# Where VectorE's transposes of K put odd and even keys in a grouped-query attention kernel

## The chip, the cores and the metric

The kernel runs on one core of a Trainium2 chip. The metric is device time in microseconds of one execution, the median of the runs shown. The engines are named as in the profile: PE is TensorE (PEld its weight loads), DVE is VectorE, ACT is ScalarE, POOL is GpSimd, and SP issues DMAs.

## The reference

Attention with 32 query heads and 8 key/value heads, batch 16, 16 query rows, 2048 keys and a head dimension of 128, all in bf16. Four query heads share one key/value head, so one key/value head serves 4 x 16 = 64 query rows.

```python
B, Hq, Hkv, Sq, Sk, D = 16, 32, 8, 16, 2048, 128
k = jnp.repeat(k, rep, axis=1)
v = jnp.repeat(v, rep, axis=1)
scores = jnp.einsum("bhqd,bhkd->bhqk", q, k) * D ** -0.5
p = softmax(scores, axis=-1)
out = jnp.einsum("bhqk,bhkd->bhqd", p, v)
```

## The kernel before

The 16 x 8 = 128 key/value heads are taken in 64 pairs (`NP`), and everything loops over the pairs. The two heads of a pair have 128 query rows together, one per partition.

**Loads.** SP issues everything in one order (line 176 K, line 184 V, line 196 Q, line 204 stores): for each pair 1 MB of K into one of six buffers `Kn`, 1 MB of V into one of eight buffers `Vb`, five pairs behind K, and the store of a finished pair twelve pairs behind. A K load waits until VectorE has transposed what the buffer held; a V load waits until TensorE has used it. In `Kn` each partition `a` holds 32 successive keys, 32 x 128 bf16, seen as 64 f32 words per key (a word is two neighbouring bf16). The key within the partition is split as (x, t, e): x is the half, t one of eight blocks, e even or odd.

**Transposes of K.** VectorE's function `kt` (line 317) transposes 32x32 blocks of these f32 words from `Kn` into `KT`, two instructions per pair of heads, one for each x, so that the head dimension comes to stand on the partitions. For each of 8 t and 2 b (which half of the head dimension) the block of 128 words in `KT` before the change is ordered (e, a, x): all even keys, then all odd keys, and within each the 32 partitions a with x alternating. One instruction writes one x, so its 32 results of a block go to every second word.

**Scores.** TensorE (line 268, and line 224 for matmuls on weights that are already loaded) multiplies Q by `KT` into `S_ps`, 2048 columns in four banks, in the column order in which `KT` has the keys. `S_ps` exists once, so the scores of the next pair wait until VectorE has emptied it. VectorE (line 333) multiplies by the negative scale, writes `Sneg` in SBUF (f32) and takes the row minimum into `nbias`.

**Exponential.** ScalarE (line 368) computes P = exp(nbias - Sneg) in bf16 with the row sum. P must have the even and the odd key of one place next to each other, because two bf16 are then taken as one f32 word and transposed together by TensorE (line 280) and copied out by ScalarE (line 378) as `PT`. Since `Sneg` has them 64 columns apart, the exponential's input is read with a step: for each of 16 blocks `n` and 64 places `y`, first e = 0, then e = 1, while the output is written in order.

**Output.** TensorE multiplies `PT` by V into `O_ps` (line 298, line 304 for the last twelve pairs), three pairs behind; ScalarE divides by the row sum (lines 391 and 395; VectorE at line 348 for the last pair), from the reciprocal that VectorE takes at line 324. Q is spread by GpSimd (line 165), transposed by TensorE (line 246) and copied by ScalarE (line 358), once in eight pairs, in four parts.

The order of the work is written out by hand in `pe_prog` and `act_prog`: scores of pair p + 1, exponential of p, output of p - 3, transposes of P of p. On VectorE the order of a pair is the evacuation of p, the reciprocal of p - 1, and the two transposes of K of p + 2; there are two buffers each of `KT`, `Sneg` and `P`. The engines wait for each other on semaphores that count: `sem_kt` the transposes of K, `sem_s` the scores, `sem_max` the evacuations, `sem_exp` the exponentials.

## Time and profile before

| | |
|---|---|
| median of 3 runs | 344.95 us (344.94 to 345.17) |
| profiled execution | 344.92 us, its span 343.1 us |
| PE busy | 312.1 us, 91% of the span |
| DVE busy | 297.6 us, 87% |
| ACT busy | 291.8 us, 85% |
| POOL busy | 30.3 us, 9% |
| DMA | 138.94 MB, mean 405 GB/s |
| HBM | 136.31 MB read, 2.10 MB written |
| granted TensorE clock | 1.00 |

The span runs from the first to the last instruction of the profiled execution; the time also holds what lies around it. A row of the page's groups names the line, the engine and the operation, what it writes and reads with the shapes, and how often; then its busy time in us and the mean ns of one; then the idle time of its engine just before such instructions and what ended most of it. In a timeline a row begins with the start and the duration in us; "x2" are two instructions shown as one row, and what stands in brackets is the idle time before it and its releaser.

### The profile page before, as it was taken

The page shows a single profiled execution, that of the slowest core. Times are in us where ns is not written, and L with a number is a line of the kernel's source. Part 1 is how long each engine was busy: PE and PEld are TensorE (multiplying, and loading weights), DVE is VectorE, ACT ScalarE, POOL GpSimd, SP SyncE. Part 2 cuts the span into 40 slices and gives each one's busy share as a digit, 9 for nine tenths or more (in the row PEclk, how much of TensorE's full clock was granted, in tenths as well). Part 3 has the DMA queues.
Part 4 walks back from the last instruction along what each step waited for, and adds up shares of the span by engine and source line. Part 5 has one row for each costly group of instructions (what it writes and reads, how often), then busy time and mean ns, then how long its engine had stood idle before and what let it go on. Part 6 is the DMA issues. An engine that isn't in the chain of part 4 may idle for free.

```text
span 343.1 us, 8217 instructions
## 1 busy us (share of the span) xinstructions
PE 312.1 (91%) x3904; PEld 189.2 (55%) x2880; DVE 297.6 (87%) x321; ACT 291.8 (85%) x404; POOL 30.3 (9%) x15
## 2 busy tenths in 40 slices
PE   0757999999999999999999999999999999887784
PEld 0413656655665575557555755665565575454354
DVE  2289989999999999999899989998999898989840
ACT  1258899999999999999999999999988899877864
POOL 4500012000400004000300004000040000000000
PEclk9999999999999999999999999999999999999999
DMA  7999999999999999999999999999999999999993
GB/s 294 429 414 415 415 411 413 414 416 417 412 418 419 413 415 417 412 420 415 412 421 414 414 416 416 415 418 417 415 412 419 419 412 420 417 413 418 410 393 126
DMA packets 37300, 138.94 MB, mean 405 GB/s; under 512 B 11408, under 2 KB 11664, under 8 KB 29072
## 3 DMA queue, kind: packets, MB, share of 16 engines
q1 hardware_dynamic: 37264, 138.42, 99.6%
q8 instruction: 27, 0.44, 0.5%
q14 instruction: 9, 0.07, 0.1%
HBM read 136.31 MB, written 2.10 MB: 403 GB/s over the span
## 4 chain that ended last, share of the span: by engine, by line
PE 83%; DMA 5%; issue 4%; DVE 3%; ACT 1%; SPq 1%; POOL 1%; DVEq 0%; ACTq 0%
PE O_ps L298 28%; PE S_ps L268 18%; PE S_ps L224 15%; PE ST_ps L280 15%; PE ST_ps L246 5%; DMA Vb<-in_v_dram 4%; DVE KT L317 2%; PE O_ps L304 2%; DMA Qn<-in_q_dram 1%; DVE Sneg L333 1%; POOL Q L165 1%; SPq L204 1%; ACT P L368 1%; SPq L184 0%; PE S_ps L304 0%
## 5 line engine op out<-in xcount | busy, mean ns | idle before, releaser
L333 DVE TENSOR_SCALAR_CACHE_REDUCE Sneg<-S_ps 128x2048 f32<-128x2048 f32 x64 | 146.2, 2285 | 25.2 <-PE S_ps L224 24.0
L368 ACT ACTIVATE P<-Sneg,nbias 128x2048 bf16<-128x2048 f32 x64 | 158.8, 2481 | 7.7 <-DVE Sneg L333 6.1
L317 DVE STREAM_TRANSPOSE KT<-Kn 128x1024 f32<-128x1024 f32 x128 | 150.9, 1218 | 10.9 <-DMA Kn<-in_k_dram 10.9
L268 PE MATMUL S_ps<-KT,QT 32*64 32x512 bf16 x1024 | 103.4, 391 | 5.5 <-DVE Sneg L333 4.7
L224 PE MATMUL S_ps<-KT,QT 32*64 32x512 bf16 x1024 | 102.0, 385 | 0.0
L298 PEld LDWEIGHTS O_ps<-Vb,PT 128*128 128x128 bf16 x832 | 77.3, 98 | 44.0 <-issue 35.7
L298 PE MATMUL O_ps<-Vb,PT 128*128 128x256 bf16 x832 | 99.9, 273 | 1.5 <-issue 1.5
L378 ACT ACTIVATE PT<-ST_ps 128x512 f32<-128x512 f32 x128 | 69.5, 595 | 6.0 <-PE ST_ps L280 4.8
L280 PE MATMUL ST_ps<-ident,P 128*128 128x128 f32 x512 | 69.0, 278 | 2.8 <-ACT P L368 2.8
L268 PEld LDWEIGHTS S_ps<-KT,QT 32*64 32x64 bf16 x1024 | 30.0, 104 | 70.4 <-issue 61.6
L280 PEld LDWEIGHTS ST_ps<-ident,P 128*128 128x128 f32 x512 | 55.1, 141 | 12.1 <-ACT P L368 9.6
L391 ACT ACTIVATE O<-O_ps,rrec 64x128 bf16<-64x128 f32 x104 | 37.7, 363 | 15.8 <-PE O_ps L298 14.7
L165 POOL COPY Q<-Qn 128x4096 bf16<-128x4096 bf16 x8 | 28.8, 3602 | 224.2 <-PE ST_ps L246 143.9
L246 PE MATMUL ST_ps<-ident,Q 128*128 128x128 f32 x128 | 20.4, 291 | 10.1 <-POOL Q L165 10.1
L358 ACT ACTIVATE QT<-ST_ps 128x512 f32<-128x512 f32 x32 | 19.3, 603 | 10.0 <-PE ST_ps L246 10.0
L246 PEld LDWEIGHTS ST_ps<-ident,Q 128*128 128x128 f32 x128 | 16.4, 150 | 10.1 <-issue 10.1
L304 PE MATMUL O_ps<-Vb,PT 128*64 128x128 bf16 x288 | 9.8, 220 | 7.2 <-issue 7.2
L304 PEld LDWEIGHTS O_ps<-Vb,PT 128*64 128x64 bf16 x288 | 8.5, 110 | 12.9 <-issue 12.9
L324 DVE RECIPROCAL rrec<-rowsum 128x1 f32<-128x1 f32 x64 | 10.1, 158 | 3.1 <-ACT P L368 3.1
L368 ACT ACTIVATION_READ_ACCUMULATOR P<-Sneg,nbias 128x1 f32 x64 | 12.2, 190 | 0.0
L395 ACT ACTIVATE O<-O_ps,rrec 128x128 bf16<-128x128 f32 x9 | 3.3, 365 | 6.6 <-PE O_ps L304 6.6
L333 DVE DVE_READ_ACCUMULATOR Sneg<-S_ps 128x1 f32 x64 | 5.3, 83 | 0.0
(12 smaller groups left out, 10.2 us busy)
## 6 DMA issues: line engine op xcount, KB each, us to landing
Kn<-in_k_dram SPq DMA_DIRECT2D x64, 1024.0 KB, 15.9
Vb<-in_v_dram SPq DMA_DIRECT2D x63, 1024.0 KB, 17.7
Qn<-in_q_dram SPq DMA_DIRECT2D x8, 256.0 KB, 15.6
out_dram<-O SPq DMA_DIRECT2D x64, 32.0 KB, 15.9
Vb<-in_v_dram SPq DMA_DIRECT2D x1, 768.0 KB, 13.0
Vb<-in_v_dram SPq DMA_DIRECT2D x1, 256.0 KB, 12.5
```

The lines of the kernel that those rows point to most:

```text
L165: gp.tensor_copy(Q4[:, :, :, :, :].rearrange("p j b r x -> p (j b) r x"), src.unsqueeze(2).to_broadcast([128, 16, 4, 64]),).then_inc(sem_q ...
L224: return pe.add_instruction(mybir.InstMatmult(name=nc.get_next_instruction_name(), engine=mybir.EngineType.PE, ins=[pe.lower_ap(rhs), pe.l ...
L246: ins = pe.transpose(dst[:, 128 * j:128 * (j + 1)], src[:, 4 * x + j, b, :], ident4[:, :])
L268: ins = pe.matmul(s_ap, w, x, start=(acc == 0), stop=(acc == 3))
L280: ins = pe.transpose(dst[:, 128 * t:128 * (t + 1)], P[p % 2][:, 128 * x:128 * (x + 1)], ident4[:, :])
L298: ins = pe.matmul(O_ps[:, 0:256], pt[:, j // 2, j % 2, :], Vb[p % NV][:, :, j, :], start=(j == 0), stop=(j == J - 1),)
L304: ins = pe.matmul(o_ap(p)[64 * g:64 * (g + 1), :], pt[:, j // 2, j % 2, 64 * g:64 * (g + 1)], Vb[p % NV][:, g, j, :], start=(j == 0), stop ...
L317: dve.transpose(KT[p % NKT][:, :].rearrange("p (t b e a x) -> p x e t b a", t=J // 2, b=2, e=2, x=2)[:, x, :, :, :, :], Kn[p % NK][:, :].b ...
L333: dve.tensor_scalar(Sneg[p % 2][:, :].rearrange("p (t h x) -> p h t x", t=8, h=2), S_ps[:, :].rearrange("p (h t x) -> p h t x", t=8, h=2), ...
L368: act.activation(P[p % 2][:, :].bitcast(BF16).rearrange("p (n y e) -> p n y e", n=16, e=2), Sneg[p % 2][:, :].rearrange("p (n e y) -> p n ...
L378: act.activation(PT[p % NPT][:, 4 * h:4 * (h + 1), :].rearrange("p t q -> p (t q)"), stage_ap(u), ACT.Copy,).then_inc(sem_ev, 1)
L391: ins = act.activation(Osb[p % NO][rows, :], O_ps[rows, 128 * g:128 * (g + 1)], ACT.Copy, scale=rrec[rows, p:p + 1])
```

## The change

The words of a block in `KT` change their order from (e, a, x) to (a, x, e): the even and the odd key of one place are now neighbours. One transpose, which has one x, thus writes the 32 results of a block to every fourth word instead of every second, and goes through its region once for e = 0 and once for e = 1; the compiled instruction writes 2 x 512 elements instead of 2 x 16 x 32. Scores and `Sneg` take the order from `KT`, so the exponential reads `Sneg` and writes `P` straight through, 2048 elements. The number and the order of the instructions on every engine, the waits and the DMAs stay as they are. TensorE's access pattern on `KT` stays too.

```diff
             def kt(p, x):
                 dve.wait_ge(sem_k[p % NK], 16 * (p // NK + 1))
                 dve.transpose(
-                    KT[p % NKT][:, :].rearrange("p (t b e a x) -> p x e t b a", t=J // 2, b=2, e=2, x=2)[:, x, :, :, :, :],
+                    KT[p % NKT][:, :].rearrange("p (t b a x e) -> p x e t b a", t=J // 2, b=2, e=2, x=2)[:, x, :, :, :, :],
                     Kn[p % NK][:, :].bitcast(F32).rearrange("p (x t e b c) -> p x e t b c", x=2, e=2, b=2, c=32)[:, x, :, :, :, :],
                 ).then_inc(sem_kt, 1)
...
                     act.activation(
-                        P[p % 2][:, :].bitcast(BF16).rearrange("p (n y e) -> p n y e", n=16, e=2),
-                        Sneg[p % 2][:, :].rearrange("p (n e y) -> p n y e", n=16, e=2), ACT.Exp,
+                        P[p % 2][:, :].bitcast(BF16), Sneg[p % 2][:, :], ACT.Exp,
                         bias=nbias[:, p:p + 1], scale=-1.0, accum_out=rowsum[:, p:p + 1],
                     ).then_inc(sem_exp, 1)
```

## The prediction

> **What bounds the kernel now.** I read the page's groups of instructions first, to see what the two edited lines cost.

> ```profile
> L333 DVE TENSOR_SCALAR_CACHE_REDUCE Sneg<-S_ps 128x2048 f32<-128x2048 f32 x64 | 146.2, 2285 | 25.2 <-PE S_ps L224 24.0
> L368 ACT ACTIVATE P<-Sneg,nbias 128x2048 bf16<-128x2048 f32 x64 | 158.8, 2481 | 7.7 <-DVE Sneg L333 6.1
> L317 DVE STREAM_TRANSPOSE KT<-Kn 128x1024 f32<-128x1024 f32 x128 | 150.9, 1218 | 10.9 <-DMA Kn<-in_k_dram 10.9
> L378 ACT ACTIVATE PT<-ST_ps 128x512 f32<-128x512 f32 x128 | 69.5, 595 | 6.0 <-PE ST_ps L280 4.8
> L391 ACT ACTIVATE O<-O_ps,rrec 64x128 bf16<-64x128 f32 x104 | 37.7, 363 | 15.8 <-PE O_ps L298 14.7
> ```

> The two VectorE rows lie on one straight line: (2285 - 1218) / 1024 = 1.042 ns an element and a fixed 151 ns. So the transposes, which now write with a step of two f32 (8 bytes), pay nothing for it that the unstepped evacuation does not pay. ScalarE's exponential is the opposite: 2481 ns for 2048 elements, while its rows for 512 and 128 elements give (595 - 363) / 384 = 0.604 ns an element.

> Next the DMA: the page's share of the queue, and the stretches by engine, whose columns are the busy time of PE, PEld, DVE, ACT and POOL, the granted clock, the DMA share and GB/s.

> ```profile
> q1 hardware_dynamic: 37264, 138.42, 99.6%
> 40.00:80.00 40.00, 40.00 (x480) 24.23 (x344) 37.72 (x41) 37.51 (x54) 3.60 (x1) 1.00 1.03 415
> 240.00:280.00 40.00, 38.49 (x457) 23.32 (x327) 36.27 (x41) 36.04 (x53) 3.60 (x1) 1.00 1.02 415
> 320.00:330.00 10.00, 7.22 (x132) 4.51 (x108) 7.31 (x9) 6.50 (x11) 0.00 (x0) 1.00 1.03 409
> ```

> The DMA engines are busy throughout at a flat 415 GB/s, and 138.42 MB at that rate take 333.5 us. TensorE has no idle time in the middle, because it starts late: its first scores come at 14.5 us. From 240 us it has idle time again, and in 320:330 it is busy for 7.22 of 10 us. It has caught up with the loads and waits for them. The timeline of the tail says the same:

> ```profile
> 326.19 1.66 SPq L189 DMA_DIRECT2D Vb<-in_v_dram  x2
> ...
> 339.30 1.09 PE L304 MATMUL S_ps<-Vb,PT 128*64 128x128 bf16 x32 [0.73 <-DMA Vb<-in_v_dram]
> 340.53 0.35 DVE L348 TENSOR_SCALAR O<-S_ps,rrec 128x128 bf16<-128x128 f32 x1 [3.92 <-PE S_ps L304]
> ```

> The last V was issued at 326.19 us and landed 13 us later, behind about 5 MB of other transfers; its matmuls waited for it, and after them come only one evacuation and one store. Today's floor is the loads. Compute lies close under it, and the third view shows how close for VectorE: the start, where it is the bound by itself.

> ```profile
> 24.87 0.16 DVE L324 RECIPROCAL rrec<-rowsum 128x1 f32<-128x1 f32 x1
> 24.94 2.35 DVE L317 STREAM_TRANSPOSE KT<-Kn 128x1024 f32<-128x1024 f32 x2
> 27.22 2.25 DVE L333 TENSOR_SCALAR_CACHE_REDUCE Sneg<-S_ps 128x2048 f32<-128x2048 f32 x1
> 29.40 0.08 DVE L333 DVE_READ_ACCUMULATOR Sneg<-S_ps 128x1 f32 x1
> 29.40 0.16 DVE L324 RECIPROCAL rrec<-rowsum 128x1 f32<-128x1 f32 x1
> ```

> From 24.87 to 29.40 VectorE never idles: one pair of KV heads costs it 4.53 us (two transposes, one evacuation, one reciprocal). In the middle TensorE sets the pace: in the chain of waits the output matmuls of successive pairs start at 140.00, 144.76, 149.41, 154.60 and 159.75 us, so 4.65 to 4.76 us a pair, or 5.15 to 5.19 us in the four of eight pairs that also transpose Q. The loads allow one pair in 333.5 / 64 = 5.21 us. VectorE therefore has 0.68 us a pair of room against the loads.

> **The change, part by part.** It adds and removes no instruction, wait or DMA, and the order on every engine stays. TensorE's reads of KT have the same addresses and the same step as before; only which key stands in which column differs. So the line-268 matmuls, the evacuation and the 32-bit transposes of P cost what they cost. Two access patterns differ.

> *The exponential* (64 times). It read two elements 64 f32 apart, then went back; now it walks straight through. Its new time is bounded by the ScalarE rows: from above by four evacuations of 512, 4 x 595 = 2380 ns, from below by 363 + 1920 x 0.604 = 1523 ns. I take the middle, 1950 ns: 0.5 us off each, 34 us of ScalarE's 292 us in all. On the path this is worth nothing: ScalarE is busy 37.5 of 40 us in the middle stage, and what it would release earlier is TensorE, which itself runs ahead of the loads from 240 us on. In the tail the last exponential ends at 336.31 us and its transposes follow, but the last matmuls stand until 339.30 us for V. Gain at the end: 0.

> *The transposes of K* (128 times). Within one instruction the 32 results of a block went to every second f32; now they go to every fourth, and the instruction passes over the whole region twice, once for even and once for odd keys. Compared by address: the 1024 results were spread over 8 KB in one pass; now there are two passes of 8 KB each, 512 results each, one per 16 bytes. No row of the trace shows a VectorE write with a 16-byte step, so this is the unknown cost, bounded from both sides. Below: 1218 ns. It can't be less, since the number of elements is the same and both VectorE rows already lie on the same 1.042 ns an element. Above: two passes at the price of the present one, 2 x 1218 = 2436 ns. The exponential is the nearest row of a stream with far-apart neighbours in SBUF: against its bounds above it pays (2481 - 2380) / 2048 = 0.05 to (2481 - 1523) / 2048 = 0.47 ns an element, in the middle 0.26. On a transpose that would be +0.05 to +0.48 us, in the middle +0.27. But that row reads, and its two interleaved streams each return to neighbouring words, four to 16 bytes; the new write never returns to a neighbour within a pass. I therefore take the upper end without the fixed part, which one instruction pays once: 151 + 2 x 1067 = 2285 ns, +1.067 us on each.

> [...]

> The cover goes quickly. With d more per transpose a pair costs VectorE 4.53 + 2d. Waiting behind a transpose are, on VectorE, the next pair's evacuation, and behind that TensorE's next scores, which wait for S_ps to be emptied, and ScalarE's exponential. The first evacuation begins at 18.17 us (the four transposes before it have 5.66 to 18.17 us, and even four of 2.285 us fit). Then 62 cycles with transposes follow. After the start of evacuation 62: that evacuation 2.25, scores of pair 63 2.2, its evacuation 2.3, exponential with its accumulator 2.2, transposes and their evacuation 1.9, matmuls 1.2, norm 0.7, store 2.2: 15 us. So the span is the larger of the loads' 343.1 us and

> 18.2 + 62 x (4.53 + 2d) + 15.

> It passes 343.1 at d = 0.23 us, a transpose of 1.45 us. For d = 1.067: 18.2 + 62 x 6.66 + 15 = 446.1 us. TensorE needs at most 5.19 us of each 6.66, and the loads 5.21, so neither is late; K loads would then wait for VectorE to free their buffers. The profiled execution took 344.92 us for a span of 343.1, so 1.8 us lie around it (the median of the runs is 344.95, the same): 447.9 us, **forecast 448 us**. The upper end of 2436 ns (d = 1.22) gives 467 us; with a tail and cycle a little shorter than mine, 445. That is this case's own range.

> **Rivals.**
> 1. *The step costs VectorE only what the exponential pays now.* d = 0.27: 18.2 + 62 x 5.07 + 15 = 347.5, 349 us; at d = 0.48, 375 us. For it: the exponential's row, the only one in the trace. Against it: that is a read that comes back to its neighbours. A transpose between 1.45 and 1.8 us would show it.
> 2. *The step costs VectorE nothing.* d = 0: the sum gives 314 us, far under the loads; time stays at 344.9 us, since the exponential's 34 us lie behind the loads. For it: the present 8-byte step is free.
> 3. *Faster: the loads flow better.* SP's queue holds its loads behind stores that wait for ScalarE: 19.2 us at the norms of line 391. With the exponential 0.5 us shorter the norms come earlier. If the DMA rate rose from 415 to the best of the middle slices, 421 GB/s, 320 us x 6 / 421 = 4.6 us would go: 340 us. It decides only while a transpose stays under 1.45 us. Against it: the queue is busy 99.6% already and 5 MB wait at the end, so earlier issue shortens no transfer.

> **How the numbers follow.** Transposes at about double, 448 us: 0.54. Rival 1, 345 to 382 us: 0.20, of which 0.02 stays within the bound for no change. Rival 2, 344.9 us: 0.18. Rival 3, 340 us: 0.08. About 0.2%, 0.7 us, is what a measurement of this kernel can tell from no change. So slower 0.54 + 0.18 = 0.72, same 0.18 + 0.02 = 0.20, faster 0.08. To hold 8 in 10 the range must reach from the unchanged case to the doubled one: 344.5 to 456 us leaves out rival 3 and the top of the doubled case, some 0.05.

> **What would show it.** The mean of the line-317 row decides: near 2285 ns for the forecast, with VectorE near 100% busy from 20 us on, pairs every 6.7 us, the DMA share falling to about 333 / 446 = 75%, and waits of SP at line 176 for the transposes. The exponential's row should be 1.5 to 2.4 us in every case; if it stays at 2481, the change does not do what it says for ScalarE. A transpose of 1218 ns with a changed time would refute the account of the loads; a slow transpose with an unchanged time would refute the VectorE sum.

## The result and the profile after

The changed kernel takes 406.94 us (median of 6 runs, 405.05 to 407.17) against 345.06 us in the same comparison: ratio 1.178, 95% interval 1.175 to 1.180, so 62 us slower. Its profiled execution took 407.02 us, with a span of 405.2 us; again 1.8 us lie around the span.

The page's group rows after the change, with the DMA queue's row ahead of them:

```profile
q1 hardware_dynamic: 37264, 138.42, 90.2%
...
DVE 71%; issue 21%; PE 5%; DMA 1%; POOL 1%; ACT 0%; SPq 0%; DVEq 0%; ACTq 0%
...
L317 DVE STREAM_TRANSPOSE KT<-Kn 128x1024 f32<-128x1024 f32 x128 | 247.1, 2003 | 5.6 <-DMA Kn<-in_k_dram 5.6
...
L333 DVE TENSOR_SCALAR_CACHE_REDUCE Sneg<-S_ps 128x2048 f32<-128x2048 f32 x64 | 145.0, 2266 | 7.2 <-PE S_ps L224 7.1
L368 ACT ACTIVATE P<-Sneg,nbias 128x2048 bf16<-128x2048 f32 x64 | 128.1, 2002 | 19.3 <-DVE Sneg L333 17.4
```

The transposes went from 1218 to 2003 ns and the exponential from 2481 to 2002 ns; the evacuation stayed. The chain that ended last, which ran through TensorE for 83% of the span before, now lies 71% in VectorE. The stretches by engine (columns PE, PEld, DVE, ACT, POOL, granted clock, DMA share, GB/s) show one engine without a gap and the loads slowed:

```profile
120.00:160.00 40.00, 32.84 (x390) 21.17 (x283) 40.00 (x35) 28.61 (x45) 3.60 (x1) 1.00 1.00 360
360.00:380.00 20.00, 14.38 (x256) 8.97 (x208) 20.00 (x17) 11.99 (x18) 0.00 (x0) 0.99 0.80 299
```

Why the loads are slow is in SP's own waits: its K loads wait for a buffer that VectorE has not yet transposed.

```profile
SPq L176 <- DVE KT L317: 260.7, 58, 10.3
```

It was 53.4 us in 24 waits before. A K load takes 5.3 us from issue to landing (median), where it took 15.9; that fits fewer transfers ahead of it in the queue.

```profile
Kn<-in_k_dram SPq DMA_DIRECT2D x64, 1024.0 KB, 5.3
```

The DMA share did not fall with the rate: it is 1.00 from 120 to 160 us at 360 GB/s, and was 1.03 before at 415. The share alone thus does not show that the loads are at their limit. VectorE's timeline gives the new cycle, from evacuation to evacuation:

```profile
30.25 2.28 DVE L333 TENSOR_SCALAR_CACHE_REDUCE Sneg<-S_ps 128x2048 f32<-128x2048 f32 x1
...
32.53 3.85 DVE L317 STREAM_TRANSPOSE KT<-Kn 128x1024 f32<-128x1024 f32 x2
36.26 2.29 DVE L333 TENSOR_SCALAR_CACHE_REDUCE Sneg<-S_ps 128x2048 f32<-128x2048 f32 x1
...
38.55 3.87 DVE L317 STREAM_TRANSPOSE KT<-Kn 128x1024 f32<-128x1024 f32 x2
42.27 2.27 DVE L333 TENSOR_SCALAR_CACHE_REDUCE Sneg<-S_ps 128x2048 f32<-128x2048 f32 x1
```

A pair takes 42.27 - 36.26 = 6.01 us, against 4.53 before. The first evacuation starts at 18.15 us and evacuation 62 at 390.31 us, so the mean of all 62 cycles is 6.00 us, and 14.9 us follow: 18.15 + 62 x 6.00 + 14.9 = 405.2 us, the whole span.

### The profile page after: what moved, and what is told of

Its sections match the earlier page's. It is cut to its first block, busy times and chain, and to the rows that moved or that the text cites. A ratio compares the mean times of both kernels' runs of the same rounds, so it can differ in the third digit from the quotient of the medians.

```text
span 405.2 us, 8217 instructions
## 1 busy us (share of the span) xinstructions
PE 318.5 (79%) x3904; PEld 199.4 (49%) x2880; DVE 384.9 (95%) x321; ACT 262.2 (65%) x404; POOL 30.3 (7%) x15
## 3 DMA queue, kind: packets, MB, share of 16 engines
q1 hardware_dynamic: 37264, 138.42, 90.2%
## 4 chain that ended last, share of the span: by engine, by line
DVE 71%; issue 21%; PE 5%; DMA 1%; POOL 1%; ACT 0%; SPq 0%; DVEq 0%; ACTq 0%
DVE KT L317 36%; DVE Sneg L333 34%; DMA Qn<-in_q_dram 1%; PE S_ps L268 1%; DVE rrec L324 1%; PE S_ps L224 1%; PE ST_ps L246 1%; POOL Q L165 1%; PE S_ps L304 1%; PE ST_ps L280 1%; PE O_ps L304 1%; ACT QT L358 0%; SPq L176 0%; DVE O L348 0%; ACT P L368 0%
## 5 line engine op out<-in xcount | busy, mean ns | idle before, releaser
L317 DVE STREAM_TRANSPOSE KT<-Kn 128x1024 f32<-128x1024 f32 x128 | 247.1, 2003 | 5.6 <-DMA Kn<-in_k_dram 5.6
L268 PE MATMUL S_ps<-KT,QT 32*64 32x512 bf16 x1024 | 111.6, 403 | 73.1 <-DVE Sneg L333 63.4
L333 DVE TENSOR_SCALAR_CACHE_REDUCE Sneg<-S_ps 128x2048 f32<-128x2048 f32 x64 | 145.0, 2266 | 7.2 <-PE S_ps L224 7.1
L368 ACT ACTIVATE P<-Sneg,nbias 128x2048 bf16<-128x2048 f32 x64 | 128.1, 2002 | 19.3 <-DVE Sneg L333 17.4
L224 PE MATMUL S_ps<-KT,QT 32*64 32x512 bf16 x1024 | 112.1, 399 | 0.0
L268 PEld LDWEIGHTS S_ps<-KT,QT 32*64 32x64 bf16 x1024 | 37.1, 106 | 138.3 <-issue 131.3
L298 PE MATMUL O_ps<-Vb,PT 128*128 128x256 bf16 x832 | 99.9, 273 | 0.0
L298 PEld LDWEIGHTS O_ps<-Vb,PT 128*128 128x128 bf16 x832 | 77.2, 98 | 42.3 <-issue 34.0
L390 ACT ACTIVATE O<-O_ps,rrec 64x128 bf16<-64x128 f32 x104 | 37.7, 363 | 89.3 <-PE O_ps L298 88.7
L280 PE MATMUL ST_ps<-ident,P 128*128 128x128 f32 x512 | 67.9, 276 | 0.9 <-ACT P L368 0.8
L280 PEld LDWEIGHTS ST_ps<-ident,P 128*128 128x128 f32 x512 | 58.1, 142 | 5.6 <-issue 2.5
L304 PEld LDWEIGHTS O_ps<-Vb,PT 128*64 128x64 bf16 x288 | 8.8, 114 | 6.6 <-issue 6.6
L368 ACT ACTIVATION_READ_ACCUMULATOR P<-Sneg,nbias 128x1 f32 x64 | 12.0, 187 | 0.0
L324 DVE RECIPROCAL rrec<-rowsum 128x1 f32<-128x1 f32 x64 | 9.5, 148 | 2.3 <-ACT P L368 2.3
L304 PE MATMUL O_ps<-Vb,PT 128*64 128x128 bf16 x288 | 10.2, 226 | 0.0
L333 DVE DVE_READ_ACCUMULATOR Sneg<-S_ps 128x1 f32 x64 | 4.7, 73 | 0.0
```

The costliest lines, as they stand in the source:

```text
L224: return pe.add_instruction(mybir.InstMatmult(name=nc.get_next_instruction_name(), engine=mybir.EngineType.PE, ins=[pe.lower_ap(rhs), pe.l ...
L268: ins = pe.matmul(s_ap, w, x, start=(acc == 0), stop=(acc == 3))
L280: ins = pe.transpose(dst[:, 128 * t:128 * (t + 1)], P[p % 2][:, 128 * x:128 * (x + 1)], ident4[:, :])
L298: ins = pe.matmul(O_ps[:, 0:256], pt[:, j // 2, j % 2, :], Vb[p % NV][:, :, j, :], start=(j == 0), stop=(j == J - 1),)
L304: ins = pe.matmul(o_ap(p)[64 * g:64 * (g + 1), :], pt[:, j // 2, j % 2, 64 * g:64 * (g + 1)], Vb[p % NV][:, g, j, :], start=(j == 0), stop ...
L317: dve.transpose(KT[p % NKT][:, :].rearrange("p (t b a x e) -> p x e t b a", t=J // 2, b=2, e=2, x=2)[:, x, :, :, :, :], Kn[p % NK][:, :].b ...
```

## The experiments

**Each half alone.** The transposes alone in the new layout:

```diff
-  KT[...].rearrange("p (t b e a x) -> p x e t b a", ...)
+  KT[...].rearrange("p (t b a x e) -> p x e t b a", ...)
   (exponential as before)
```

> Only the transposes' new layout; the exponential keeps its old pattern, so the keys it puts together are not those that V expects. Theory (VectorE sets the pace, ScalarE's gain is off the path): transposes near 2003 ns, exponential near 2481 ns, a pair every 6.0 us, time 407 us as with the whole change. Rival (the shorter exponential gave time back in the changed kernel): up to 62 x 0.48 = 30 us more, 437 us.

Measured: 406.88 us (median), ratio 1.179 (1.177 to 1.181). VectorE's timeline in the profiled run:

```profile
30.93 3.85 DVE L317 STREAM_TRANSPOSE KT<-Kn 128x1024 f32<-128x1024 f32 x2
...
36.90 3.86 DVE L317 STREAM_TRANSPOSE KT<-Kn 128x1024 f32<-128x1024 f32 x2
...
42.89 3.88 DVE L317 STREAM_TRANSPOSE KT<-Kn 128x1024 f32<-128x1024 f32 x2
```

The pairs are 5.97 and 5.99 us apart, and the exponential takes 2502 ns. The mean of the transposes is 2194 ns here, not the 2003 expected: in this profile all VectorE records lengthen in the course of the run, the accumulator reads as well (269 ns in the mean, 83 before the change), while the starts keep their distance, 5.99 us in the mean of all 62 cycles. Why the records lengthen is open; the distance is what is used here. The whole loss comes from the transposes, and the 0.48 us that each exponential saves gives nothing back: 406.88 with the slow one, 406.94 with the fast one.

The exponential alone read straight through:

```diff
   (transposes as before)
-  P[...].bitcast(BF16).rearrange("p (n y e) -> p n y e", n=16, e=2),
-  Sneg[...].rearrange("p (n e y) -> p n y e", n=16, e=2), ACT.Exp,
+  P[...].bitcast(BF16), Sneg[...], ACT.Exp,
```

> Only the exponential reads straight through; the transposes stay, so even and odd keys are not brought together as V expects. Theory (the loads are the floor): exponential 2002 ns, transposes 1218 ns, time 345 us within 0.7. Rival 3 of the prediction (the loads flow better when the stores wait less): 340 us.

Measured: 344.99 us, ratio 0.9994 (0.9985 to 1.0003). The group rows:

```profile
L317 DVE STREAM_TRANSPOSE KT<-Kn 128x1024 f32<-128x1024 f32 x128 | 151.2, 1220 | 16.6 <-DMA Kn<-in_k_dram 16.0
L333 DVE TENSOR_SCALAR_CACHE_REDUCE Sneg<-S_ps 128x2048 f32<-128x2048 f32 x64 | 145.9, 2280 | 20.3 <-PE S_ps L224 20.2
L368 ACT ACTIVATE P<-Sneg,nbias 128x2048 bf16<-128x2048 f32 x64 | 128.2, 2003 | 7.1 <-DVE Sneg L333 5.7
L390 ACT ACTIVATE O<-O_ps,rrec 64x128 bf16<-64x128 f32 x104 | 37.7, 362 | 42.4 <-PE O_ps L298 41.8
```

ScalarE works 31 us less and the time does not move. ScalarE's idle time in front of the norms (the division by the row sum), where it waits for TensorE's output matmuls, grows from 15.8 to 42.4 us; VectorE's wait for K loads in front of the transposes grows from 10.9 to 16.0 us. Is TensorE the floor, then, rather than the loads? Before, it was busy without a gap from 180 to 240 us. Here it is not (columns as above):

```profile
180.00:240.00 60.00, 56.53 (x670) 35.66 (x483) 54.02 (x57) 47.73 (x74) 3.60 (x1) 1.00 1.03 416
```

TensorE catches up with the loads sooner and has 3.5 us of idle time in this stretch, the DMA rate is the 416 GB/s of before, and the end stays where it was: the loads are the floor. SP's waits for the norms of `O_ps` fell from 19.2 to 14.8 us, as rival 3 had it, but the rate did not rise and the time did not fall. Rival 3 is refuted.

**How much slower transposing the loads would hide.** Every second or every fourth pair in the changed form, the others as before (the change in words):

```diff
+  KT in "(t b a x e)" order and the exponential straight if p % K4 == 0, else as before   # K4 = 4, 2
```

> Every fourth pair in the changed form (transposes and exponential), the others as before. Theory (larger of the loads' floor and 18.2 + 62 c + 15, c = mean VectorE cycle = 4.53 + 0.25 x 1.47 = 4.90 us): the sum gives 337 us, under the loads' 343.1, so the slow transposes are hidden and the time stays at 345 us. Rival (each slow transpose costs its length at the end): a quarter of the loss, 345 + 62 / 4 = 360 us.

> Every second pair in the changed form. Theory: c = 4.53 + 0.5 x 1.47 = 5.27 us, 18.2 + 62 x 5.27 + 15 + 1.8 = 361 us. Rival (each slow transpose costs its length): half the loss, 376 us.

Measured: 347.90 us with every fourth pair (ratio 1.0064, 1.0040 to 1.0089), 364.25 us with every second (1.0551, 1.0527 to 1.0576). Both lie far from the rival's 360 and 376 us, but somewhat above the theory: the first 2.9 us above the expected 345, the second 2.5 us above its sum, 18.2 + 62 x 5.27 + 15 + 1.8 = 361.7 us. Of the ten runs of the first, four took 345.53 to 345.85 us, as expected, and six 347.81 to 348.68 us. What parts them is open. The profile is of one of the six, 348.54 us; VectorE's timeline in it:

```profile
201.10 2.25 DVE L335 TENSOR_SCALAR_CACHE_REDUCE Sneg<-S_ps 128x2048 f32<-128x2048 f32 x1
...
206.10 2.29 DVE L335 TENSOR_SCALAR_CACHE_REDUCE Sneg<-S_ps 128x2048 f32<-128x2048 f32 x1 [0.39 <-PE S_ps L225]
...
211.19 2.29 DVE L335 TENSOR_SCALAR_CACHE_REDUCE Sneg<-S_ps 128x2048 f32<-128x2048 f32 x1 [0.44 <-PE S_ps L225]
213.48 3.94 DVE L318 STREAM_TRANSPOSE KT<-Kn 128x1024 f32<-128x1024 f32 x2
217.24 2.30 DVE L335 TENSOR_SCALAR_CACHE_REDUCE Sneg<-S_ps 128x2048 f32<-128x2048 f32 x1
```

Before 206.10 and 211.19 VectorE waits for TensorE's scores; the pair with the slow transposes, 211.19 to 217.24, then costs 6.05 us, which VectorE sets. So VectorE sets some pairs here and TensorE others. Eight pairs, 190.52 to 231.00 us, take 40.48 us, 5.06 a pair where the mean of VectorE's own cycles is 4.90; 18.2 + 62 x 5.06 + 15 = 346.9 us, beside the measured span of 346.8. The threshold that the prediction set at a cycle of 5.00 us thus holds in this profile for the cycle that results, not for the mean of VectorE's work. With every second pair the profile has 5.31 us in the mean of 62 cycles, where the sum had 5.27, and 15.4 us after them.

**What in the write is slow.** A stretch is here four f32 words side by side, 16 bytes. The step of the write varied from pair to pair (the change in words); the sixth form keeps 4 words but writes the even and the odd half of each block in turn, not in two passes over the region.

```diff
-  KT as "(t b e a x)"
+  KT as "(t b e x a)", "(t b e a x)", "(t b a x e)", "(t a b x e)", "(u a v b x e)" for p % 6 = 0 to 4
+  KT as "(t b a x e)", iterated t e b a instead of e t b a, for p % 6 = 5
```

> The transposes of K write with steps of 1, 2, 4, 8 and 16 words by turns of the pair, and every sixth pair with 4 words but the even and odd halves of each block written one after the other instead of in two passes over the whole region; the keys come out in other columns, so only durations count. Theory A (a result pays when it does not share its 16-byte stretch with its neighbour): 1218, 1218, 2003, 2003, 2003 ns, and 2003 for the sixth. Theory B (the address walked is paid, as the prediction's doubling supposed): 2003 at step 4, and more at each doubling, 3.5 us at 8. Theory C (the second pass over words already half written is what costs): the sixth form, which comes back after 64 results, differs from 2003.

Measured: 380.29 us in one run. The transposes of pairs 0 to 5 in VectorE's timeline, two to a row, with steps of 1, 2, 4, 8, 16 and the sixth form:

```profile
5.65 2.37 DVE L327 STREAM_TRANSPOSE KT<-Kn 128x1024 f32<-128x1024 f32 x2 [5.65 <-DMA Kn<-in_k_dram]
9.36 2.37 DVE L327 STREAM_TRANSPOSE KT<-Kn 128x1024 f32<-128x1024 f32 x2 [1.33 <-DMA Kn<-in_k_dram]
...
20.39 3.85 DVE L327 STREAM_TRANSPOSE KT<-Kn 128x1024 f32<-128x1024 f32 x2
...
26.58 3.93 DVE L327 STREAM_TRANSPOSE KT<-Kn 128x1024 f32<-128x1024 f32 x2
...
32.63 3.65 DVE L327 STREAM_TRANSPOSE KT<-Kn 128x1024 f32<-128x1024 f32 x2
...
38.67 3.85 DVE L327 STREAM_TRANSPOSE KT<-Kn 128x1024 f32<-128x1024 f32 x2
```

The later turns of the six forms repeat these rows within 0.1 us. Theory A holds. Steps of 1 and 2 words are alike, from 4 words on the price is there and does not grow, and the order of the two halves changes nothing. The address walk, with which the prediction reasoned, is refuted: a step of 8 words walks twice as far as 4 and costs the same.

**Is it the transposing?** The evacuation, which transposes nothing, writes with the same steps:

```diff
-  Sneg[...].rearrange("p (t h x) -> p h t x", ...), S_ps[...].rearrange("p (h t x) -> p h t x", ...)
+  Sneg[...].rearrange("p (m s) -> p s m", s=STEPS[p % 5]), S_ps[...].rearrange("p (s m) -> p s m", s=STEPS[p % 5])   # 1, 2, 4, 8, 16
```

> The evacuation writes Sneg with steps of 1, 2, 4, 8 and 16 words by turns of the pair, which permutes the keys; only durations count. If the price belongs to every VectorE write: 2270, 2270, then 2270 + 2048 x 0.77 = 3840 ns from step 4 on, and a time near 374 us. If it belongs to the transposing alone: 2270 at all steps and 345 us.

Measured: 387.0 us in one run; the first five evacuations:

```profile
18.17 2.29 DVE L334 TENSOR_SCALAR_CACHE_REDUCE Sneg<-S_ps 128x2048 f32<-128x2048 f32 x1 [6.97 <-PE S_ps L225]
24.28 2.29 DVE L334 TENSOR_SCALAR_CACHE_REDUCE Sneg<-S_ps 128x2048 f32<-128x2048 f32 x1 [1.53 <-PE S_ps L225]
28.85 3.77 DVE L334 TENSOR_SCALAR_CACHE_REDUCE Sneg<-S_ps 128x2048 f32<-128x2048 f32 x1
36.37 3.87 DVE L334 TENSOR_SCALAR_CACHE_REDUCE Sneg<-S_ps 128x2048 f32<-128x2048 f32 x1 [1.48 <-PE S_ps L225]
42.45 3.64 DVE L334 TENSOR_SCALAR_CACHE_REDUCE Sneg<-S_ps 128x2048 f32<-128x2048 f32 x1
```

The price belongs to the write, not to the transposing: 3840 ns was expected from step 4 on. The time is 13 us above the 374 us expected, which took only VectorE's mean work; as with every fourth pair, waits for TensorE come on top (19.6 us in front of the evacuations in this profile, against 7.1 in the changed kernel).

**Does a read pay too?** The exponential reads `Sneg` with these steps:

```diff
-  P[...].bitcast(BF16).rearrange("p (n y e) -> p n y e", n=16, e=2), Sneg[...].rearrange("p (n e y) -> p n y e", n=16, e=2), ACT.Exp,
+  P[...].bitcast(BF16).rearrange("p (s m) -> p s m", s=STEPS[p % 5]), Sneg[...].rearrange("p (m s) -> p s m", s=STEPS[p % 5]), ACT.Exp,   # 1, 2, 4, 8, 16
```

> The exponential reads Sneg with steps of 1, 2, 4, 8 and 16 words by turns of the pair, which permutes the keys; only durations count. If reads pay by the same 16-byte stretches: 2002 at steps 1 and 2, and from 4 on more, between the 2481 ns of the old alternating pattern and 2002 + 2048 x 0.77 = 3570 ns. If the old pattern's price came from its short runs of two alone: 2002 at all steps. Time 345 us, up to 355 at the upper end.

Measured: 384.87 us in one run; the first five exponentials:

```profile
18.86 2.00 ACT L369 ACTIVATE P<-Sneg,nbias 128x2048 bf16<-128x2048 f32 x1 [4.51 <-DVE Sneg L334]
23.34 2.18 ACT L369 ACTIVATE P<-Sneg,nbias 128x2048 bf16<-128x2048 f32 x1 [0.55 <-DVE Sneg L334]
27.88 3.98 ACT L369 ACTIVATE P<-Sneg,nbias 128x2048 bf16<-128x2048 f32 x1 [0.43 <-DVE Sneg L334]
34.15 4.04 ACT L369 ACTIVATE P<-Sneg,nbias 128x2048 bf16<-128x2048 f32 x1
40.62 3.79 ACT L369 ACTIVATE P<-Sneg,nbias 128x2048 bf16<-128x2048 f32 x1
```

Reads pay as well, and more than the bracket allowed: 1.98 us over the straight read, not at most 1.57. So did the time. The exponentials average 3.19 us here, and with ScalarE's other work of a pair (0.19 + 0.74 + 1.09 + 0.30) that is 5.5 us, above the loads' 5.21; ScalarE became the bound and TensorE waited 47.6 us for it. The expectation had capped the slow read with VectorE's surcharge per element instead of its rate. In ns an element the two agree: (2003 - 151) / 1024 = 1.81 for the transposes, (3870 - 151) / 2048 = 1.82 for the evacuation, (3980 - 293) / 2048 = 1.80 for the exponential. Its fixed part of 293 ns comes from the exponential's run below, where one of 2 elements takes 295 ns: (2002 - 295) / 2046 = 0.83 ns an element, and 295 - 2 x 0.83 = 293. VectorE and ScalarE have different rates on straight data (1.04 and 0.83 ns) and the same one here.

**A stretch or a threshold?** Steps of 2, 3, 4 and 6 words, where 3 words (12 bytes) tell three models apart (the changes in words):

```diff
+  s = STEPS[p % 4]; m = 2048 // s                  # 2, 3, 4, 6
+  columns s*m to 2048 in a short instruction; columns 0 to s*m with "p (m s) -> p s m" on Sneg
```

> The evacuation writes Sneg with steps of 2, 3, 4 and 6 words by turns of the pair (where 2048 is not a multiple, the last two columns by a short instruction of their own), which permutes the keys; only durations count. Model S (a 16-byte stretch costs 1.81 ns however many neighbours share it, and an element at least 1.04 ns): 2 words 2.29 us; 3 words, 0.75 stretches an element, 0.15 + 2048 x 1.36 = 2.93 us; 4 and 6 words 3.86 us. Model T (a threshold: a step under 16 bytes is free, from 16 on the rate is 1.81 ns): 2.29, 2.29, 3.86, 3.86 us. Model U (every step beyond 8 bytes pays in full): 2.29, 3.86, 3.86, 3.86 us.

> The exponential reads Sneg with steps of 2, 3, 4 and 6 words by turns of the pair (the last two columns by a short instruction where needed), which permutes the keys; only durations count. Model S (1.80 ns a stretch, at least 0.83 ns an element, 0.30 us fixed): 2 words 0.30 + 2048 x 0.90 = 2.14 us; 3 words 0.30 + 2048 x 1.35 = 3.06 us; 4 and 6 words 3.98 us. Model T: 2.18, 2.18, 3.98, 3.98 us. Model U: 2.18, 3.98, 3.98, 3.98 us.

Measured: 385.03 and 397.78 us in one run each. Evacuations of pairs 4 to 7, then exponentials of pairs 4 to 7:

```profile
40.99 2.28 DVE L338 TENSOR_SCALAR_CACHE_REDUCE Sneg<-S_ps 128x2048 f32<-128x2048 f32 x1
46.15 2.98 DVE L338 TENSOR_SCALAR_CACHE_REDUCE Sneg<-S_ps 128x2046 f32<-128x2046 f32 x1
51.35 3.88 DVE L338 TENSOR_SCALAR_CACHE_REDUCE Sneg<-S_ps 128x2048 f32<-128x2048 f32 x1
57.50 3.84 DVE L338 TENSOR_SCALAR_CACHE_REDUCE Sneg<-S_ps 128x2046 f32<-128x2046 f32 x1
```

```profile
44.51 2.15 ACT L374 ACTIVATE P<-Sneg,nbias 128x2048 bf16<-128x2048 f32 x1
...
50.13 3.06 ACT L374 ACTIVATE P<-Sneg,nbias 128x2046 bf16<-128x2046 f32 x1
55.63 4.03 ACT L374 ACTIVATE P<-Sneg,nbias 128x2048 bf16<-128x2048 f32 x1
...
61.81 3.96 ACT L374 ACTIVATE P<-Sneg,nbias 128x2046 bf16<-128x2046 f32 x1
```

The short exponential of 2 elements, from the groups of the exponential's run:

```profile
L372 ACT ACTIVATE P<-Sneg,nbias 128x2 bf16<-128x2 f32 x32 | 9.4, 295 | 0.7
```

Model S fits all eight: 2.93 us was expected at 3 words for VectorE and 3.06 for ScalarE, 2.98 and 3.06 came. T and U are refuted by that step. The rule that these runs show, for f32 streams in SBUF with one fixed step, written by VectorE or read by ScalarE: 1.8 ns for every 16-byte stretch that the stream comes to, or the engine's own time per element, whichever is more. VectorE's reads, ScalarE's writes and other types were not measured. Nor does the rule cover a stream that alternates between two places: the exponential before the change comes to another stretch at every element, which by the rule would be 0.30 + 2048 x 1.80 = 3.99 us, and it took 2.48. Two words a stretch give 0.90 ns an element, which VectorE's 1.04 covers and ScalarE's 0.83 doesn't, hence 2.15 to 2.18 us there instead of 2.00.

**A version with neither price.** The evacuation brings even and odd keys together, with a write step of 2 words, and the transposes stay as they were:

```diff
-  Sneg[...].rearrange("p (t h x) -> p h t x", t=8, h=2), S_ps[...].rearrange("p (h t x) -> p h t x", t=8, h=2)
+  Sneg[...].rearrange("p (t h y e) -> p t h e y", t=8, h=2, e=2), S_ps[...].rearrange("p (h t e y) -> p t h e y", t=8, h=2, e=2)
   (transposes as before, exponential straight)
```

> The transposes stay as before the change; the even and odd keys are brought together in the evacuation's write (step 2 words, 8 bytes) and the exponential reads straight through. Theory: evacuation 2285 ns, transposes 1218, exponential 2002, time 345 us within 0.7, because the loads are the floor. Rival 3 of the prediction: 340 us. If the evacuation's write of even and odd runs costs what the old exponential's read did (0.23 ns an element): 2760 ns, a pair 5.0 us, 345 to 347 us.

Measured: 345.0 us, ratio 0.9996 (0.9987 to 1.0005). The group rows:

```profile
L317 DVE STREAM_TRANSPOSE KT<-Kn 128x1024 f32<-128x1024 f32 x128 | 151.0, 1218 | 13.9 <-DMA Kn<-in_k_dram 13.8
L333 DVE TENSOR_SCALAR_CACHE_REDUCE Sneg<-S_ps 128x2048 f32<-128x2048 f32 x64 | 146.2, 2285 | 21.7 <-PE S_ps L224 21.5
L368 ACT ACTIVATE P<-Sneg,nbias 128x2048 bf16<-128x2048 f32 x64 | 128.2, 2003 | 8.1 <-DVE Sneg L333 6.7
```

It has everything that the change wanted from ScalarE at no price on VectorE, and is not faster: the loads are the floor. No version here beats the kernel before.

## Why the prediction was right, and where its size was off

**The floor.** That the loads set the time before, and that the exponential's gain is worth nothing, held: the exponential alone gave 0.9994, and the version with all of ScalarE's gain and no cost 0.9996. The DMA share of 99.6%, which the prediction leaned on, is the weaker sign, as the 1.00 at 360 GB/s shows; the flat rate and TensorE's idle time are the stronger ones.

**The exponential's new time.** 1950 ns was taken from between bounds of 1523 and 2380; it is 2002. That the middle came so near was luck: the 0.604 ns an element of the lower bound, taken from two rows of copies, is not the exponential's, which has 0.83.

**The VectorE sum.** Its form held: start 18.15 us (18.2 in the sum), tail 14.9 us (15), every cycle of VectorE end to end. TensorE and the loads followed VectorE as foreseen, with SP's waits for the transposes at 260.7 us. One sign did not come: the DMA share was to fall to about 75%, and the queue's row has 90.2%, though its bytes at 415 GB/s would fill only 333.5 / 405.2 = 82% of the span.

**The mis-sized term: d, the extra time of one transpose.** The prediction took 1.067 us, a doubled stream, from the idea that two passes over 8 KB cost twice one pass. The row shows 2003 - 1218 = 0.785 us, and between evacuations, where successive records overlap a little, (6.00 - 4.53) / 2 = 0.735. The difference of 0.332 us in 124 transposes is 41 us, the whole distance between the forecast span of 446.1 and the measured 405.2. What stood in its place is the 1.8 ns a stretch: the stream goes from 1.04 to 1.81 ns an element, a factor of 1.74, since the old step had two results in each 16-byte stretch, by that figure 0.90 ns each and under VectorE's own 1.04 (steps of 1 and 2 words took the same 2.37 us for two transposes). The address walk gave the right direction for a wrong reason. No single case of the prediction gives 407 us: Rival 1's sums from rows end at 375 us and the doubled transposes stand at 448. The measured time lies in the gap between them, within the range only because that reached from the unchanged time to 456 us. No run shows the 382 us at which rival 1's chance ends, or the 1.8 us for its transpose; in their place came 2003 ns a transpose, 74% more an element (1.04 to 1.81 ns), and 407 us.

**Rival 1** leaned on the exponential's old pattern, (2481 - 293) / 2048 = 1.07 ns an element. That pattern alternates between two places and comes back to each stretch at the next element but one, and was no measure for a stream that does not come back within a pass; the prediction said so, and the run with a step of 4 words shows 1.80 ns for the same instruction. Rival 2 fell with the row of 2003 ns.

What stays open: why steps of 16 words are a little cheaper than 4 or 8 (3.64 against 3.77 to 3.87 us in the evacuation, 3.79 against 3.98 to 4.04 in the exponential), and what the old alternating read pays, 2.48 us where the rule for fixed steps would give 3.99.

## What to carry to other kernels

Where a layout has to put a fixed step somewhere in f32 data in SBUF, count the 16-byte stretches to which VectorE's write or ScalarE's read comes, at 1.8 ns each in these runs, and put the step where two or more elements share a stretch: here 2 words cost VectorE nothing, ScalarE 0.15 to 0.18 us for 2048 elements, and 4 words cost VectorE 0.77 ns an element. Before taking time off an engine, ask what it waits for when it is done: ScalarE's 31 us only lengthened waits under the floor of the loads, while VectorE had 0.68 us a pair of room and the change took 1.47. Where two engines take turns as the bound, a sum of one engine's mean work is too low: with every fourth pair it gave 337 us for a profiled span of 346.8.

## What the runs showed of the hardware that was not expected

A slow start passed to the end only where the loads no longer covered it. In the profile of the changed kernel each group of four of the first scores' matmuls took 0.64 to 0.66 us and the first evacuation began at 18.15 us; in that of the transposes alone they took 0.42 us and it began at 16.62 us, and the spans are 405.2 and 403.6 us. Under the floor of the loads the same difference cost nothing: the first evacuation began at 18.17 us in the kernel before and at 16.57 us with the exponential alone, and both spans are 343.1 us. Why the start differs was not shown.
